# Three low-half subtractions and their sources moved from VectorE and PSUM to GpSimd and SBUF in a recurrence followed by two gated MLPs

## The chip, the cores and the metric

The kernel runs on one core of a Trainium2 chip. The metric is device microseconds of one execution, and a kernel's time is the median of its runs. The engines go by the profile's names: PE is TensorE, DVE is VectorE, ACT is ScalarE, POOL is GpSimd, SP issues most of the DMAs. A name ending in q (SPq, ACTq) is an engine's own instruction queue.

## The reference

```python
state = zeros(B, H, D, D)                       # B, H, S, D = 4, 8, 768, 40
for t in range(S):
    y[t] = einsum('bhd,bhde->bhe', r[t], state)
    Sa = einsum('bhde,bhe->bhd', state, a[t])
    state = state * w[t][:, :, None, :] - outer(Sa, b[t]) + outer(v[t], k[t])
x = y as (3072, 320)
h = x @ w_in                                    # 320 -> 2048
g = where(h >= 1, h, where(h <= -1, 0, (h + 1)**2 / 4))
x = g @ w_out                                   # 2048 -> 320
out = (silu(x @ w_gate) * (x @ w_val)) @ w_out2 # 320 -> 1536 -> 320
```

All inputs and the output are f32.

## The kernel before

**Halves.** TensorE is fed f16. Each f32 operand is cut in a high part (a cast, made by ScalarE) and a low part (the f32 value less the high part, rounded to f16), and three of the four products of halves are summed in f32. So nearly every value that goes into a product costs one copy on ScalarE and, after it, one subtraction on VectorE or GpSimd. GpSimd does it only where the f32 value is in SBUF; where it is in PSUM, VectorE does.

**Chunks.** The 768 time steps are cut into 12 chunks (c = 0 to 11) of 64, and the recurrence of a chunk is turned into matrix products. A unit n = 4c + j is one chunk of one batch element j, with its 8 heads side by side, so there are 48 units. A unit has two parts:
- `p_tasks` (line 821) prepares: loads a, r, k, b and the running products of the decay w, multiplies, splits, transposes, and multiplies keys with a and b (`mm`, line 883) into a PSUM tile pg of 128 x 512 f32. Rows 0 to 63 are masked in place to the strictly triangular part (line 889, VectorE), cast to the f16 high part in lkt (line 904, ScalarE) and subtracted to its low part (line 910, VectorE). Rows 64 to 127 are copied to the SBUF tile gf (line 893) and go through DRAM to the inversion.
- `m_tasks` (line 1011) runs the recurrence: scales v by 256 into its f16 high part vh (line 1053) and makes its low part into vss (line 1057, VectorE by the helper `split`, line 569, 128 x 320); then alternates products and splits (`mm_x`, `mm_sa`, `mm_c`) through a PSUM tile px; transposes vss; multiplies with r (`mm_q`, line 1149) into pg; masks that in place (line 1155, VectorE), casts its high part into wt (line 1159, ScalarE), subtracts its low part into wt (line 1161, VectorE by line 567, 128 x 512); `mm_y` (line 1165) then gives the output y and the next state, which the same unit of the next chunk needs (tiles s0t, s0s). The output is transposed into mx (`turn_x`, line 1006).

`inv_tasks` (line 919) inverts all small triangular blocks of a chunk on VectorE in 62 dependent pairs of steps (lines 949 and 954), in a pg tile that it holds all that while. `decay_tasks` makes the running products of w, for four chunks at a time.

**The MLPs.** Four units of a chunk make 256 tokens. `in1` (8 pieces a chunk) and `in2` (6 pieces) multiply with the input weights (line 1218, PSUM tile ph), apply the activation on ScalarE and VectorE, split the result (line 1238 on ScalarE, then line 1240 on GpSimd by `split`, line 567), and `outp` multiplies with the output weights (line 1285, PSUM tile po). The weights come in as f32 pieces while the kernel runs; `wpiece` (line 612) turns each with three bit operations on VectorE (lines 641, 645, 651), a scaling and a cast on ScalarE (lines 671, 663) and a low-part subtraction on GpSimd or, for the narrow pieces, VectorE. They share buffers (wr, wu) in SBUF.

**What sets the order.** Nothing is written in final order. Every step is handed to `Plan.task` (line 45) with an engine, a cost, what it reads and writes, the buffers that it uses and a priority. `Plan.forward` (line 69) plays the program through with these costs, each engine taking the ready task of best priority, a buffer going to the next user when its last one is done; `Plan.backward` (line 220) does so from the end to get priorities; `Plan.run` (line 320) goes between them `rounds` times and then emits each engine's instructions in the order of the last pass. So every engine's queue has a fixed order made at build time, in which an instruction waits for its inputs and all behind it wait too. Tables of offsets to the priorities by chunk, unit and step (`K.nudge`, `K.last`, lines 1328 to 1430) shape that order. `lk=True` marks VectorE tasks that the planner doesn't play beside a GpSimd task. The numbers of buffers matter here: pg has two PSUM tiles, gf, wt, ldv, ss one each, vh two, vss three; sr, a staging tile for the next state, lies in rows 0 to 39 of gf.

The sets KLP, VLP, L2P, ARP, XSP (lines 382 to 386) name the chunks in which a low part is made by GpSimd (`side`, line 575, picks engine and cost); VLP is empty.

Of the kernel before, what the change touches and what calls it, by code (L numbers as in the profile page):

```python
# [15 lines left out]
class Plan:  # L16
# [10 lines left out]
    def __init__(self):  # L27
        self.tasks, self.made, self.pools, self.slots = [], {}, {}, {}
        self.bias, self.unit, self.nudge, self.last = 0.0, ["z", 0, 0], ({}, {}), ({}, {})
        self.lim, self.rounds, self.loose = 0.73, 2, ()  # L30
# [38 lines left out]
    def forward(self, prio):  # L69
# [59 lines left out]
        while done < len(ts):  # L129
            started = True  # L130
            while started:
                started = False
                for eng in self.ENGINES[:5]:
# [7 lines left out]
                    while any(heaps):  # L141
# [42 lines left out]
                        if t["dma"]:  # L184
                            heapq.heappush(events, (end, -1))
                            dma = max(dma, begin) + t["dma"]
                            end = dma + 1.79
# [32 lines left out]
    def backward(self, prio):  # L220
# [16 lines left out]
        def lat(t):  # L237
            return 1.16 + t["dma"] if t["dma"] else t["lat"]
# [107 lines left out]
def tile_recurrence__then__gated_mlps(  # L346
# [36 lines left out]
    VLP = ()  # L383
    L2P = range(12)
    ARP = range(1, 12)
    XSP = range(12)
    VO = 1
# [58 lines left out]
    K.pool("sr", [gfs[0][0:D].bitcast(F16).rearrange("p h t -> p (h t)")[:, 0:3 * HD].rearrange(  # L446
        "p (l h d) -> p l h d", l=3, h=H)])
    sbt("pf", [128, H, C], F32, 1)
    mx = sbt("mx", [128, 36 * NT], F16)
# [82 lines left out]
    def c_v(n, ps=False):  # L532
        return 0.15 + n * 1.04e-3
# [19 lines left out]
    def hc(ap):  # L553
        return ap.rearrange("p (h t) -> p h t", h=H)
# [266 lines left out]
    def p_tasks(n, p):  # L821
# [61 lines left out]
        def mm():  # L883
# [4 lines left out]
        T("PE", 0.3, mm, r=[(key, "kbT"), ("art", n)], w=[(key, "g")], use=PG + KT + A_ + GF + LK + L2, p=p)  # L888
        T("DVE", c_v(512, True), lambda: v_.tensor_tensor(
            out=hc(G("pg", key))[0:C], in0=hc(G("pg", key))[0:C],  # L890
            in1=mask[0:C].unsqueeze(1).to_broadcast([C, H, C]), op=ALU.mult),
          r=[(key, "g")], w=[(key, "gm")], use=PG, p=p)
# [9 lines left out]
        for hf in range(2):  # L902
            DMA(lambda e, hf=hf: st(e, hf), r=[(key, "gf")], w=[("lsd", c)], use=GF, p=p - 20, dma=0.24, cost=0.68)
        T("ACT", c_s(512), lambda: s_.copy(
            out=G("lkt", key)[0:C, 0:H], in_=hc(G("pg", key))[0:C]),
          r=[(key, "gm")], w=[(key, "lkh")], use=PG + LK, p=p)
# [3 lines left out]
        T("DVE", c_v(512), lambda: v_.tensor_tensor(  # L910
            out=G("lkt", key)[C:128, 0:H], in0=hc(G("pg", key))[0:C],
            in1=G("lkt", key)[0:C, 0:H], op=ALU.subtract), r=[(key, "lkh")], w=[("lk", n)], use=PG + LK, p=p)
# [98 lines left out]
    def m_tasks(n, p):  # L1011
# [15 lines left out]
        if j % 2 == 0:  # L1027
# [24 lines left out]

        T("ACT", c_s(HD), lambda: s_.activation(
            out=G("vh", key), in_=G("ldv", mp)[:, j % 2], func=AF.Copy, scale=2.0**8),
          r=[(mp, "v")], w=[(key, "vh")], use=V + VH, p=p - 1)
        e0, eng, cost = side(c in VLP, HD)
        T(eng, cost, lk=True, emit=lambda: split(
            G("vss", key)[:, :, D:2 * D], G("ldv", mp)[:, j % 2], 2.0**8, G("vh", key), e0),
# [90 lines left out]
        def mm_q():  # L1149
# [4 lines left out]
        T("PE", 0.28, mm_q, r=[(key, "vsT"), ("art", n)], w=[(key, "q")], use=PQ + VT + AT, p=p)  # L1154
        T("DVE", c_v(512, True), lambda: v_.tensor_tensor(
            out=hc(G(pg, (key, "q"))), in0=hc(G(pg, (key, "q"))),
            in1=mask.unsqueeze(1).to_broadcast([128, H, C]), op=ALU.mult),
          r=[(key, "q")], w=[(key, "pf")], use=PQ, p=p)
        T("ACT", c_s(512), lambda: s_.copy(out=G("wt", key)[:, 0, :, 0:C], in_=hc(G(pg, (key, "q")))),
          r=[(key, "pf")], w=[(key, "ph")], use=PQ + WT, p=p)  # L1160
        T("DVE", c_v(512), lambda: split(
            G("wt", key)[:, 1, :, 0:C], hc(G(pg, (key, "q"))), 1.0, G("wt", key)[:, 0, :, 0:C]),
          r=[(key, "ph")], w=[(key, "wt")], use=PQ + WT, p=p)
# [161 lines left out]
    def by(tables):  # L1325
# [248 lines left out]
```

## Time and profile before

| | us |
|---|---|
| median of 3 runs | 1077.28 |
| lowest, highest run | 1075.42, 1082.75 |
| the profiled execution | 1082.65 |
| its span, first to last instruction | 1080.6 |

| engine | busy us | share of the span | instructions |
|---|---|---|---|
| PE | 886.9 | 82% | 10944 |
| DVE | 760.4 | 70% | 1901 |
| ACT | 715.4 | 66% | 1336 |
| POOL | 691.1 | 64% | 912 |

The profiled execution is one run with the hardware profiler on; its span is what the trace shows, and about 2 us lie around it. A busy share is a mean over stretches with different limits, so the rows below go by stretches. PEclk is the clock that TensorE was granted, as a share of full speed. A wait is the idle time of an engine just before an instruction, put down to what came last.

### The profile page before, as it was taken

The numbers are of one execution on the slowest core, as the hardware profiler recorded it, in microseconds if no ns is written. First come the engines' busy times: TensorE is split into PE (matmuls) and PEld (weight loads), VectorE is DVE, ScalarE is ACT, GpSimd is POOL, SyncE is SP. The second block draws the span as 40 slices with busy tenths as digits, with TensorE's granted clock in tenths as the row PEclk, the third lists the DMA queues.
The fourth block names the chain that finished last, engine by engine and source line by source line (L and its number), as shares of the span: only waits on it lengthen the run. The fifth ranks groups of instructions, "written<-read, shape, count | busy, mean of one in ns | idle before, by whom it ended". The sixth has DMA issues, their size and how long they took to land.

```text
span 1080.6 us, 28683 instructions
## 1 busy us (share of the span) xinstructions
PE 886.9 (82%) x10944; PEld 732.9 (68%) x10944; DVE 760.4 (70%) x1901; ACT 715.4 (66%) x1336; POOL 691.1 (64%) x912
## 2 busy tenths in 40 slices
PE   0421326648886999999999999999999999999998
PEld 0311325436764787887878878888888888888887
DVE  8688897999998586884965967848769478441211
ACT  1785676668875967777758768677687674643422
POOL 4588885666887767776766667767668564432222
PEclk9999967769997999999999999999999999999999
DMA  7976798679897897498795875978959462230000
GB/s 224 198 196 158 208 193 178 170 176 230 206 203 143 167 166 136 101 161 151 151 123 119 147 150 115 148 134 161 140 122 162 97 121 58 58 43 20 14 3 25
DMA packets 386193, 147.93 MB, mean 137 GB/s; under 512 B 344536, under 2 KB 362776, under 8 KB 386056
## 3 DMA queue, kind: packets, MB, share of 16 engines
q1 hardware_dynamic: 360118, 133.63, 59.8%
q10 hardware_dynamic: 25938, 12.47, 6.0%
q8 instruction: 86, 1.41, 0.6%
q14 instruction: 51, 0.42, 0.1%
HBM read 78.25 MB, written 21.52 MB: 92 GB/s over the span
## 4 chain that ended last, share of the span: by engine, by line
PE 47%; DVE 26%; DMA 9%; ACT 6%; issue 5%; POOL 3%; SPq 2%; ACTq 0%; DVEq 0%; POOLq 0%
PE ph L1218 25%; PE po L1285 15%; DVE ub L949 3%; DVE pg L954 3%; DVE vss L569 3%; PE pg L1173 2%; DMA tt<-tsd 2%; DVE px L641 1%; DMA mx<-x 1%; DVE mx L1254 1%; PE px L1084 1%; DVE px L645 1%; PE px L1073 1%; PE px L1091 1%; DVE xs L569 1%
## 5 line engine op out<-in xcount | busy, mean ns | idle before, releaser
L1285 PE MATMUL po<-wo,mx 128*128 128x320 f16 x2016 | 314.5, 304 | 11.1 <-ACT wo L663 5.8
L567 POOL TENSOR_TENSOR mx<-mx 128x512 f16<-128x512 f32 x168 | 195.6, 1167 | 175.0 <-ACT mx L1238 168.3
L1285 PEld LDWEIGHTS <-mx 128*128 128x128 f16 x2016 | 191.6, 99 | 80.9 <-issue 7.1
L1218 PE MATMUL ph<-mx,w 128*128 128x256 f16 x1536 | 190.7, 277 | 20.0 <-DMA mx<-x 10.0
L1218 PEld LDWEIGHTS <-w 128*128 128x128 f16 x1536 | 150.0, 99 | 44.7 <-issue 19.5
L1254 DVE SCALAR_TENSOR_TENSOR mx<-ph,mx 128x512 f32<-128x512 f32 x96 | 66.2, 689 | 109.1 <-ACT mx L1251 105.3
L1218 PE MATMUL ph<-x2t,wv 128*128 128x256 f16 x1152 | 141.3, 272 | 1.4 <-DVE mx L1268 1.4
L1218 PE MATMUL ph<-x2t,wg 128*128 128x256 f16 x1152 | 140.3, 272 | 2.2 <-ACT mx L1265 2.2
L1238 ACT CAST mx<-mx 128x512 f16<-128x512 f32 x168 | 102.5, 613 | 54.7 <-DVE mx L1268 29.9
L1218 PEld LDWEIGHTS <-wg 128*128 128x128 f16 x1152 | 110.0, 98 | 17.4 <-issue 2.7
L1218 PEld LDWEIGHTS <-wv 128*128 128x128 f16 x1152 | 109.3, 98 | 14.6 <-issue 1.4
L954 DVE TENSOR_TENSOR pg<-pg,ub 128x126 f32<-128x126 f32 (+22 forms) x372 | 95.7, 257 | 8.2
L949 DVE SCALAR_TENSOR_TENSOR ub<-ub,pg 128x126 f32<-128x126 f32 (+22 forms) x372 | 92.0, 247 | 10.9 <-DMA ub<-lsd 1.1
L1268 DVE SCALAR_TENSOR_TENSOR mx<-ph,mx 128x512 f32<-128x512 f32 x72 | 49.5, 687 | 67.0 <-PE ph L1218 65.5
L1250 ACT ACTIVATE mx<-ph 128x512 f32<-128x512 f32 x96 | 57.1, 595 | 35.4 <-PE ph L1218 32.0
L1116 ACT ACTIVATE vss<-px 32x640 f16<-32x640 f32 x90 | 60.8, 690 | 18.9 <-PE px L1084 14.0
L573 POOL TENSOR_TENSOR ldp<-ldp 128x640 f32<-128x640 f32 (+1 forms) x46 | 70.6, 1545 | 2.6 <-ACT ldp L853 0.6
L1265 ACT ACTIVATE mx<-ph 128x512 f32<-128x512 f32 x72 | 42.7, 594 | 42.8 <-PE ph L1218 38.6
L1107 POOL COPY xs<-xs 32x320 f16<-32x320 f16 x93 | 41.4, 449 | 40.4 <-ACT xs L1102 36.6
L1251 ACT ACTIVATE mx<-mx 128x512 f32<-128x512 f32 x96 | 60.5, 630 | 3.1
L1084 PEld LDWEIGHTS <-tt 96*128 96x128 f16 (+1 forms) x768 | 28.1, 96 | 41.4 <-DMA tt<-tsd 15.0
L569 DVE SCALAR_TENSOR_TENSOR vss<-px,vss 32x320 f16<-32x320 f32 x90 | 43.5, 484 | 16.9 <-ACT vss L1116 13.8
(232 smaller groups left out, 1684.3 us busy)
## 6 DMA issues: line engine op xcount, KB each, us to landing
ub<-lsd SPq DMA_DIRECT2D x24, 256.0 KB
ldp<-in_kb_dram SPq DMA_DIRECT2D x19, 320.0 KB
ldv<-in_v_dram SPq DMA_DIRECT2D x19, 320.0 KB
ldp<-in_ar_dram SPq DMA_DIRECT2D x18, 320.0 KB
wo<-in_wo_dram SPq DMA_DIRECT2D x16, 320.0 KB
waf<-was SPq DMA_DIRECT2D x23, 160.0 KB
out_dram<-mx SPq DMA_DIRECT2D x23, 160.0 KB
ldp<-wks SPq DMA_DIRECT2D x20, 160.0 KB
```

Of the source, the lines that this page charges most:

```text
L567: e.tensor_tensor(out=out, in0=x, in1=hi, op=ALU.subtract)
L569: e.scalar_tensor_tensor(out=out, in0=x, scalar=scale, in1=hi, op0=ALU.mult, op1=ALU.subtract)
L573: e.tensor_tensor(out=out, in0=x, in1=y, op=ALU.mult)
L949: v_.scalar_tensor_tensor(out=t, in0=L()[:, j, j + 1:].unsqueeze(1).to_broadcast([128, nm, ni]), scalar=-(2.0**-10), in1=m[:, 0:nm, j:j + ...
L954: v_.tensor_tensor(out=m[:, 0:nm, j + 1:], in0=m[:, 0:nm, j + 1:], in1=t, op=ALU.add)
L1116: s_.activation(out=hi2(G("vss", key)[z]), in_=two(hd(G("px", key))[32 * hf:32 * hf + 32]), func=AF.Copy, scale=-(2.0**-10))
L1218: t_.matmul(out=ps, lhsT=wts[:, wi, fs], rhs=xT[:, xi, :], start=(i == 0), stop=(i == len(plan) - 1))
L1238: T("ACT", c_s(512) - 0.04, lambda: s_.copy(out=G("g", key)[:, 0], in_=u2(key)), r=[(key, "u")], w=[(key, "gh")], use=U + GG, p=p)
L1250: s_.activation(out=u2(key), in_=ps2(key), func=AF.Relu, scale=2.0**-8, bias=1.0)
L1251: s_.activation(out=u2(key), in_=u2(key), func=AF.Square, scale=2.0**3)
L1254: T("DVE", c_v(512, True), lambda: v_.scalar_tensor_tensor(out=u2(key), in0=ps2(key), scalar=2.0**8, in1=u2(key), op0=ALU.max, op1=ALU.min ...
L1285: t_.matmul(out=ps, lhsT=g[:, x, f, 128 * tt:128 * tt + 128], rhs=wo[:, 2 * i + f, y, :], start=(n == 1 and f == 0 and m == 0), stop=(n == ...
```

## The change

The low part of v (chunks 1 to 11), of the masked key product (chunks 2 to 11) and of the masked r product (chunks 1 to 11) is made by GpSimd in place of VectorE. GpSimd can't take the masked products from PSUM, so VectorE's mask multiplication writes them to SBUF (rows 0 to 63 of gf; a new tile qf of 128 x 512 f32), and ScalarE's cast reads them there. For v, ScalarE multiplies the loaded pair of units by 256 in place, once for two units, so that the low part is a plain subtraction. The staging tile sr moves from gf to unused rows of ss. Beside that, the planner's numbers change: `lim` 0.73 to 1.13, `rounds` 2 to 4, two DMA latencies, and all four tables of offsets are replaced.

```diff
--- before.py
+++ after.py
@@ -27,7 +27,7 @@
     def __init__(self):
         self.tasks, self.made, self.pools, self.slots = [], {}, {}, {}
         self.bias, self.unit, self.nudge, self.last = 0.0, ["z", 0, 0], ({}, {}), ({}, {})
-        self.lim, self.rounds, self.loose = 0.73, 2, ()
+        self.lim, self.rounds, self.loose = 1.13, 4, ()
 
     def pool(self, name, tiles):
         self.pools[name] = dict(free=list(tiles), users={}, spares=[], grow=[])
@@ -184,7 +184,7 @@
                         if t["dma"]:
                             heapq.heappush(events, (end, -1))
                             dma = max(dma, begin) + t["dma"]
-                            end = dma + 1.79
+                            end = dma + 1.94
                         else:
                             end += t["lat"]
                         heapq.heappush(events, (end, i))
@@ -235,7 +235,7 @@
         now, done, starts, held, events, size = 0.0, 0, [0.0] * len(ts), set(), [], len(ts)
 
         def lat(t):
-            return 1.16 + t["dma"] if t["dma"] else t["lat"]
+            return 1.44 + t["dma"] if t["dma"] else t["lat"]
 
         seen = set()
 
@@ -380,10 +380,12 @@
     NDC = 2
     NPM = 1
     KLP = range(1, 12)
-    VLP = ()
+    VLP = range(1, 12)
     L2P = range(12)
     ARP = range(1, 12)
     XSP = range(12)
+    WTP = range(1, 12)
+    LKP = range(2, 12)
     VO = 1
     WSP = True
     NW1 = 14
@@ -443,9 +445,10 @@
     sbt("xs", [128, H, D], F16, 2)
     tts = sbt("tt", [128, 4 * H * HC + C], F16, 1)
     gfs = sbt("gf", [128, H, C], F32, 1)
-    K.pool("sr", [gfs[0][0:D].bitcast(F16).rearrange("p h t -> p (h t)")[:, 0:3 * HD].rearrange(
+    K.pool("sr", [ss[0][0:D].rearrange("p h t -> p (h t)")[:, 0:3 * HD].rearrange(
         "p (l h d) -> p l h d", l=3, h=H)])
     sbt("pf", [128, H, C], F32, 1)
+    sbt("qf", [128, H, C], F32, 1)
     mx = sbt("mx", [128, 36 * NT], F16)
     K.pool("xt", [mx[:, 6 * NT * i:6 * NT * (i + 1)].rearrange("p (a t) -> p a t", a=6)
                   for i in range(2)])
@@ -886,10 +889,13 @@
                 t_.matmul(out=ps[:, h], lhsT=kT[0:120, h, :], rhs=at[0:120, h, 0:C])
 
         T("PE", 0.3, mm, r=[(key, "kbT"), ("art", n)], w=[(key, "g")], use=PG + KT + A_ + GF + LK + L2, p=p)
+        lkp = c in LKP
+        gm = lambda: G("gf", key)[0:C] if lkp else hc(G("pg", key))[0:C]
+        GM = GF if lkp else PG
         T("DVE", c_v(512, True), lambda: v_.tensor_tensor(
-            out=hc(G("pg", key))[0:C], in0=hc(G("pg", key))[0:C],
+            out=gm(), in0=hc(G("pg", key))[0:C],
             in1=mask[0:C].unsqueeze(1).to_broadcast([C, H, C]), op=ALU.mult),
-          r=[(key, "g")], w=[(key, "gm")], use=PG, p=p)
+          r=[(key, "g")], w=[(key, "gm")], use=PG + GM, p=p)
         T("ACT", c_s(512), lambda: s_.activation(
             out=G("gf", key)[C:128], in_=hc(G("pg", key))[C:128], func=AF.Copy, scale=2.0**-6),
           r=[(key, "g")], w=[(key, "gf")], use=PG + GF, p=p)
@@ -901,15 +907,15 @@
 
         for hf in range(2):
             DMA(lambda e, hf=hf: st(e, hf), r=[(key, "gf")], w=[("lsd", c)], use=GF, p=p - 20, dma=0.24, cost=0.68)
-        T("ACT", c_s(512), lambda: s_.copy(
-            out=G("lkt", key)[0:C, 0:H], in_=hc(G("pg", key))[0:C]),
-          r=[(key, "gm")], w=[(key, "lkh")], use=PG + LK, p=p)
+        T("ACT", c_s(512), lambda: s_.copy(out=G("lkt", key)[0:C, 0:H], in_=gm()),
+          r=[(key, "gm")], w=[(key, "lkh")], use=GM + LK, p=p)
         T("ACT", c_s(256), lambda: s_.copy(
             out=G("l21", key)[64:96, 1:1 + H], in_=G("gf", key)[64:96, :, HC:C]),
           r=[(key, "gf")], w=[(key, "l2h")], use=GF + L2, p=p)
-        T("DVE", c_v(512), lambda: v_.tensor_tensor(
-            out=G("lkt", key)[C:128, 0:H], in0=hc(G("pg", key))[0:C],
-            in1=G("lkt", key)[0:C, 0:H], op=ALU.subtract), r=[(key, "lkh")], w=[("lk", n)], use=PG + LK, p=p)
+        e3, eng, cost = side(lkp, 512)
+        T(eng, cost, lambda: e3.tensor_tensor(
+            out=G("lkt", key)[C:128, 0:H], in0=gm(),
+            in1=G("lkt", key)[0:C, 0:H], op=ALU.subtract), r=[(key, "lkh")], w=[("lk", n)], use=GM + LK, p=p)
         e2, eng, cost = side(c in L2P, 256)
         T(eng, cost, lk=True, emit=lambda: split(
             G("l21", key)[96:128, 1:1 + H], G("gf", key)[64:96, :, HC:C], 1.0,
@@ -1050,12 +1056,19 @@
                 out=tiles(64, 96), in_=td[0].rearrange("s f b t -> s f (b t)")),
                 r=[("tsd", c)], w=[(mp, "tt")], use=TT, p=p - 3, dma=0.25, cost=0.68)
 
+        vscale = 2.0**8
+        if c in VLP:
+            vscale = 1.0
+            if j % 2 == 0:
+                T("ACT", c_s(2 * HD), lambda: s_.activation(
+                    out=G("ldv", mp), in_=G("ldv", mp), func=AF.Copy, scale=2.0**8),
+                  r=[(mp, "v")], w=[(mp, "v8")], use=V, p=p - 2)
         T("ACT", c_s(HD), lambda: s_.activation(
-            out=G("vh", key), in_=G("ldv", mp)[:, j % 2], func=AF.Copy, scale=2.0**8),
-          r=[(mp, "v")], w=[(key, "vh")], use=V + VH, p=p - 1)
+            out=G("vh", key), in_=G("ldv", mp)[:, j % 2], func=AF.Copy, scale=vscale),
+          r=[(mp, "v8" if c in VLP else "v")], w=[(key, "vh")], use=V + VH, p=p - 1)
         e0, eng, cost = side(c in VLP, HD)
         T(eng, cost, lk=True, emit=lambda: split(
-            G("vss", key)[:, :, D:2 * D], G("ldv", mp)[:, j % 2], 2.0**8, G("vh", key), e0),
+            G("vss", key)[:, :, D:2 * D], G("ldv", mp)[:, j % 2], vscale, G("vh", key), e0),
           r=[(key, "vh")], w=[(key, "vl")], use=V + VH + VS, p=p - 1)
         copy, eng, cost = (p_.tensor_copy, "Pool", c_ps(2 * HD)) if c >= VO else (s_.copy, "ACT", c_s(2 * HD))
         T(eng, cost, emit=lambda: copy(
@@ -1152,15 +1165,18 @@
                 t_.matmul(out=ps[:, h], lhsT=vT[0:120, h, :], rhs=at[0:120, h, C:128])
 
         T("PE", 0.28, mm_q, r=[(key, "vsT"), ("art", n)], w=[(key, "q")], use=PQ + VT + AT, p=p)
+        wtp = c in WTP
+        qm = lambda: G("qf", key) if wtp else hc(G(pg, (key, "q")))
+        QM = [("qf", key)] if wtp else PQ
         T("DVE", c_v(512, True), lambda: v_.tensor_tensor(
-            out=hc(G(pg, (key, "q"))), in0=hc(G(pg, (key, "q"))),
+            out=qm(), in0=hc(G(pg, (key, "q"))),
             in1=mask.unsqueeze(1).to_broadcast([128, H, C]), op=ALU.mult),
-          r=[(key, "q")], w=[(key, "pf")], use=PQ, p=p)
-        T("ACT", c_s(512), lambda: s_.copy(out=G("wt", key)[:, 0, :, 0:C], in_=hc(G(pg, (key, "q")))),
-          r=[(key, "pf")], w=[(key, "ph")], use=PQ + WT, p=p)
-        T("DVE", c_v(512), lambda: split(
-            G("wt", key)[:, 1, :, 0:C], hc(G(pg, (key, "q"))), 1.0, G("wt", key)[:, 0, :, 0:C]),
-          r=[(key, "ph")], w=[(key, "wt")], use=PQ + WT, p=p)
+          r=[(key, "q")], w=[(key, "pf")], use=PQ + QM, p=p)
+        T("ACT", c_s(512), lambda: s_.copy(out=G("wt", key)[:, 0, :, 0:C], in_=qm()),
+          r=[(key, "pf")], w=[(key, "ph")], use=QM + WT, p=p)
+        e4, eng, cost = side(wtp, 512)
+        T(eng, cost, lambda: split(G("wt", key)[:, 1, :, 0:C], qm(), 1.0, G("wt", key)[:, 0, :, 0:C], e4),
+          r=[(key, "ph")], w=[(key, "wt")], use=QM + WT, p=p)
 
         def mm_y():
             ps, wq, kb, at = hd(G(pg, (key, "y"))), G("wt", key), G("kbs", pk), G("art", pk)
@@ -1326,106 +1342,91 @@
         return {(u, i): x for u, table in tables.items() for i, x in table.items()}
 
     by_chunk = by({
-        "a": {9: -0.16, 10: 2.53, 11: -1.57},
...
+        "z": {0: 16.32},
...
```


## Rows read from the trace of the kernel before

**Rows 1.** Busy time of the engines in five stretches of the span, us.

```profile
core 0: us, PE busy (x) PEld busy (x) DVE busy (x) ACT busy (x) POOL busy (x), PEclk, DMA share, GB/s
0.00:160.00 160.00, 41.21 (x592) 34.60 (x593) 134.90 (x387) 99.02 (x167) 115.57 (x228) 0.94 0.80 196
160.00:340.00 180.00, 124.61 (x1524) 97.88 (x1524) 162.81 (x384) 129.37 (x248) 124.83 (x154) 0.82 0.82 191
340.00:372.00 32.00, 28.88 (x337) 23.06 (x336) 17.35 (x39) 26.08 (x48) 26.41 (x36) 0.96 0.76 144
372.00:840.00 468.00, 454.94 (x5926) 380.39 (x5924) 349.62 (x879) 344.09 (x656) 334.70 (x397) 1.00 0.77 141
840.00:1080.00 240.00, 237.24 (x2572) 197.00 (x2569) 95.74 (x216) 116.81 (x221) 89.61 (x100) 1.00 0.24 48
```

**Rows 2.** The same columns, the second stretch cut in two.

```profile
160.00:196.00 36.00, 20.09 (x216) 16.03 (x216) 27.83 (x70) 20.89 (x40) 21.81 (x36) 0.74 0.91 194
196.00:340.00 144.00, 104.52 (x1309) 81.85 (x1308) 134.99 (x315) 108.48 (x209) 103.03 (x118) 0.84 0.80 191
```

**Rows 3.** VectorE's groups by shape, 160 to 340 us: operation, count, busy us, mean ns.

```profile
L569 DVE SCALAR_TENSOR_TENSOR vss<-ldv,vh 128x320 f16<-128x320 f32 x8 | 6.2, 779 | 0.4 <-DMA vsT<-vss 0.3
...
L567 DVE TENSOR_TENSOR wt<-pg,wt 128x512 f16<-128x512 f32 x8 | 5.5, 685 | 0.1
...
L910 DVE TENSOR_TENSOR lkt<-pg,lkt 64x512 f16<-64x512 f32 x7 | 4.8, 684 | 0.9 <-ACT lkt L904 0.7
```

**Rows 4.** VectorE's groups by shape, 0 to 160 us.

```profile
L910 DVE TENSOR_TENSOR lkt<-pg,lkt 64x512 f16<-64x512 f32 x8 | 5.4, 683 | 1.3 <-ACT lkt L904 1.1
...
L910 DVE TENSOR_TENSOR lsp<-pg,lsp 64x512 f16<-64x512 f32 x2 | 1.4, 684 | 1.1 <-ACT lsp L904 1.0
```

**Rows 5.** The tile ldv: one operation's shortest, median and longest ns.

```profile
L569 DVE SCALAR_TENSOR_TENSOR vss<-ldv,vh x48: 473/675/2681, 21.8 to 939.8; 128x320 f16<-128x320 f32 x48
```

**Rows 6.** Groups of the whole span: operation, count, busy us, mean ns, idle before.

```profile
L567 POOL TENSOR_TENSOR mx<-mx 128x512 f16<-128x512 f32 x168 | 195.6, 1167 | 175.0 <-ACT mx L1238 168.3 <-POOL vss L1098 2.5 <-issue 1.2
...
L567 POOL TENSOR_TENSOR ars<-ldp,ars 128x320 f16<-128x320 f32 x44 | 35.5, 807 | 8.7 <-ACT ars L865 4.5 <-issue 1.8 <-POOL vss L1098 0.5
...
L1238 ACT CAST mx<-mx 128x512 f16<-128x512 f32 x168 | 102.5, 613 | 54.7 <-DVE mx L1268 29.9 <-DVE mx L1254 14.6 <-DMA x2t<-mx 4.9
...
L865 ACT ACTIVATE ars<-ldp 128x640 f16<-128x640 f32 x45 | 33.0, 733 | 5.7 <-POOL ldp L573 4.5 <-DMA art<-ars 0.6
...
L569 DVE SCALAR_TENSOR_TENSOR xs<-px,xs 32x320 f16<-32x320 f32 x89 | 42.5, 482 | 13.4 <-ACT xs L1102 11.1
...
L1254 DVE SCALAR_TENSOR_TENSOR mx<-ph,mx 128x512 f32<-128x512 f32 x96 | 66.2, 689 | 109.1 <-ACT mx L1251 105.3 <-PE px L1084 1.8 <-PE pg L1173 1.5
...
L1155 DVE TENSOR_TENSOR pg<-pg,mask 128x512 f32<-128x512 f32 x44 | 30.5, 693 | 2.3 <-PE pg L1152 1.9
...
L1159 ACT CAST wt<-pg 128x512 f16<-128x512 f32 x44 | 25.7, 584 | 15.9 <-DVE pg L1155 15.2
```

**Rows 7.** What TensorE waited for, 160 to 340 us: total us, times, longest.

```profile
PE po L1285 <- ACT wo L663: 5.8, 1, 5.8
...
PE pg L1173 <- DVE wt L567: 3.7, 2, 3.1
...
PE pg L886 <- DVE wt L567: 2.7, 1, 2.7
```

**Rows 8.** Line 1007's transposes into mx: first and last start, us.

```profile
L1007 SPq DMA_TRANSPOSE mx<-x x24: 1211/1244/2527, 144.3 to 971.3; - x24
```

**Rows 9.** The chain of waits: start us, us, what.

```profile
168.00 3.58 PE ph L1218 x16
...
1063.73 3.49 PE ph L1218 x32
...
1067.23 1.63 PE po L1285 x12
```

**Rows 10.** What GpSimd waited for, 372 to 840 us.

```profile
POOL mx L567 <- ACT mx L1238: 45.5, 29, 7.5
```

More of the change, by code (lines that the diff above doesn't have):

```diff
@@ L1328, in tile_recurrence__then__gated_mlps @@
     by_chunk = by({
[22 rows of a table removed]
+        "a": {0: 0.7, 11: -0.75},
+        "b": {3: 0.07, 5: -0.15, 7: 1.48, 8: -0.07, 10: 2.42, 11: 7.11},
+        "d": {0: 5.17, 1: 4.15, 2: 3.13},
+        "i": {0: -2.35, 1: -1.77, 2: -1.74, 3: -0.61, 4: 2.98, 6: 1.13, 7: 3.24, 8: 2.28, 9: 3.28, 10:
+            7.81, 11: 4.67},
+        "o": {0: 49.18},
+        "p": {15: 0.02, 16: 0.55, 17: 0.02, 18: 0.02, 19: 0.02, 20: 0.02},
+        "v": {3: 0.77, 16: 0.81, 17: 0.81},
+        "w": {0: 0.8, 1: 0.03, 2: -0.74, 3: -1.52, 4: -2.29, 5: -3.06, 6: -3.84, 7: -4.61},
+        "z": {0: 16.32},
     })
     by_step = by({
[14 rows of a table removed]
[12 rows of a table added]
     })
```

160 rows, old and new, of tables (by_chunk, by_step) are left out of this document.

## The prediction

> **What bounds the kernel now.** I read the busy times by stretch first, because the page's shares (PE 82%, DVE 70%) are means over stages with different limits. From 372 us to the end TensorE is the bound: it is busy 454.9 of 468 us and then 237.2 of 240 [rows 1], and the chain of waits there is its own matmuls [rows 9]. All that any other engine can still give back there is 468 - 454.9 = 13.1 us, and 2.8 after it. From 160 to 340 us TensorE is busy only 124.6 of 180 us, at a granted clock of 0.82; the time lost is 55 us. There VectorE is the fullest engine, 162.8 of 180, and cut in two it has 27.8 of 36 and then 135.0 of 144, 94% [rows 1, 2]. ACT has 72%, GpSimd 69%, the DMA engines 82%. So in that stretch the work that feeds TensorE (the recurrence of chunks 1 and 2, the weights of the second MLP, the inversions) goes at VectorE's pace. TensorE's longest wait there, 5.8 us for a weight cast in wo [rows 7], is of this kind: ACT had that cast to make late, because VectorE's bit operations on the piece came late in a full queue. From 0 to 160 us VectorE is busy 134.9, but the change moves almost nothing there, as chunk 0 keeps its form.
>
> The end of the kernel is therefore the point at which TensorE becomes full, plus matmul work that the change leaves alone. What is won ahead of 340 us is won at the end, and what is won on VectorE after 372 us is worth next to nothing.
>
> **The change, part by part.** The sum goes against the profiled execution, 1082.65 us (span 1080.6 and 2.05 around it). It lies 5.4 above the median of the runs, at their upper end, so I take the difference from the median, 1077.28.
>
> *VectorE loses, ahead of 340 us.* The low part of v: 8 instructions, 6.2 us. The low part of the masked r product: 8, 5.5 us. The low part of the masked key product: 7, 4.8 us [rows 3]. Before 160 us there are 10 of the last kind [rows 4], of which 8 belong to chunks 0 and 1 and stay; 2 x 0.684 = 1.4 us. Together 17.9 us. In the fullest part VectorE has only 6% of idle time to swallow this, so I count 17 us of it as time.
>
> The low part of v takes 0.779 us each there, from 0.473 to 2.681 over the kernel [rows 5], where a subtraction as wide with one operand in PSUM takes 0.482 [rows 6]. I count the 0.779 as freed, since the queue behind it stood still for that long. The Trainium skill (SBUF — State Buffer, "Who interferes with whom") says that a VectorE instruction with two SBUF inputs and a GpSimd instruction that reads SBUF lock each other out, the later one waiting for the whole of the other; the trace agrees with it in the 2.681 us. By that rule the surplus is real queue time; at the unblocked 0.482 the 17.9 would be 15.5.
>
> *GpSimd gains.* A two-input subtraction of 512 takes it 1.167 us, of 320 it takes 0.807 [rows 6]. Ahead of 340 us that is 8 x 0.807 + 17 x 1.167 = 26.3 us, nearly all after 160: its share goes from 69% to some 83%. It has the room. But two of the three are on chains: wt is what `mm_y` waits for, and each is 1.167 - 0.685 = 0.48 us longer, plus a wait in a fuller queue, for which I take half an instruction, 0.6 us. Eight units make 8.6 us if every one is on the path. TensorE had idle time before the r product's consumer put down to the wt low part for 3.7 us in 2 waits, and for the pg tile that it frees in one of 2.7 [rows 7], so about 3 of 8 units count: 3.2 us. Bounds: 0 and 8.6.
>
> *VectorE's masks* now write to SBUF in place of PSUM. A 128 x 512 instruction from PSUM to SBUF takes 0.689 and one from PSUM to PSUM 0.693 [rows 6]: nothing.
>
> *ScalarE.* Its casts read SBUF: 0.613 against 0.584 [rows 6], 15 x 0.03 = 0.4 us. The scaling of v in place is a new 128 x 640 instruction; the nearest row is 0.733 [rows 6]; 4 pairs ahead of 340 us make 2.9 us. ScalarE has 50 us idle in the stretch and v is loaded well ahead, so both cost nothing; if that cover went, 3.3 us.
>
> *Buffers.* A pg tile is free after its mask and one copy, no longer after a cast and a subtraction: earlier by 0.58 + 0.68 us. That is worth from nothing to the 2.7 us of the wait named above; I take half, 1.3. Against it, gf (one tile) is held until GpSimd has made the key's low part, where it was held until its two DMAs to DRAM had read it; the next unit's key product waits for gf. Mask, cast and subtraction make 0.69 + 0.58 + 1.17 = 2.4 us after the product, and the same time runs for the copy and the DMAs, so I take nothing; at worst it is 7 x 0.6 = 4 us. The staging tile sr leaves gf, which takes a user off it. ldv (one pair) and vh wait for GpSimd where they waited for VectorE: 0.03 us more per instruction, plus its queue.
>
> *DMAs* stay the same in number and size; SP issues the same.
>
> *The new order.* All tables and two constants of the planner change, so every queue is ordered anew. No row shows a price. Its upper end is what a better order could find: 160 - 134.9 = 25.1 us of VectorE idle time before 160 us, of which half, 12.5, might be had, and some of the 13.1 after 372. Its lower end I take at the same 13.1 us lost. I put it at nothing and keep both ends for the range.
>
> Sum: -17 + 3.2 - 1.3 = -15. The profiled execution would become 1068 and the median **1062**.
>
> **The rivals.**
>
> *GpSimd becomes the pace (slower).* From 372 to 840 us it is busy 334.7 of 468 [rows 1]. Of the 44, 44 and 40 units of the three kinds, 36, 36 and 31 are left after 340 us; they take 36 x 0.807 + 67 x 1.167 = 107 us and lie between 340 and 971, where the recurrence ends [rows 8], so 468/631 of them, 80 us, fall in that stretch: 414 of 468, 89%. The 133 us that it idles now are not all free: 45.5 of them it waits for the f16 cast that its own MLP subtraction needs [rows 10]. If it can use only a third of them, 44, it falls 36 us behind, and the outcome is -15 + 36: 1098. The point of decision is a share of 85%, (334.7 + 80 - 15) / 468: if its queue can't get beyond that, the loss eats the whole gain. For it: every one of TensorE's output products waits for a GpSimd subtraction. Against it: the last transpose of the recurrence starts 109 us before the end, while chunk 11's own MLPs take 8 x (1.75 + 1.63) + 6 x (3.49 + 1.63) = 58 us by the durations of [rows 9]. TensorE has 51 us of other work in hand by then, so a recurrence that falls back by less than that leaves it full; and after 840 us GpSimd has only 89.6 of 240 to do. VectorE ran at 94% in order, so 89% can be had. The Trainium skill (GPSIMD Engine Reference, "Engine selection") advises against just this move: elementwise work belongs on VectorE, as GpSimd is about 2 times slower with two inputs. The rows have 1.167 against 0.685, 1.7 times. By the rule the move is a loss of engine time, and it is one of time here only if this rival holds. Chance 0.13.
>
> *VectorE is not what paces the stretch (no change).* The loads of the weights and the decays, 82% of the DMA engines [rows 1], or the recurrence's own latency would then set the time, and VectorE would only idle more. The chain loses 3.2 us more, the order gives or takes a few: 1071 to 1083, centre 1078. For it: the first 36 us of the stretch have the DMA engines at 0.91 and VectorE at 77% [rows 2]. Against it: the 94% of the 144 us after. Chance 0.27.
>
> *The new order pays by itself (faster still).* With half of the 25.1 us before 160: 1062 - 12.5 = 1050. Chance 0.10.
>
> **How the numbers follow.** My forecast has 0.50, with a range of its own of 1056 to 1071: 17.9 with no loss on the chains against 17.9 x 0.9 with 8.6 lost. The likeliest time is 1062. The 8 in 10 range is 1047 to 1082: it leaves out the slower case (0.13) and the low half of the last one (0.05). A measurement of this kernel tells about 1% from no change, so the borders are 1066.5 and 1088. Faster: 0.42 of the forecast's 0.50, the 0.10, and 0.01 of the flat case, 0.53. Same: 0.08, 0.26 and 0.01 of the slow case, 0.35. Slower: 0.12.
>
> **What would show it.** VectorE's busy time should fall by 34 + 30 + 27 us (44 units at 0.779, 44 at 0.685, 40 at 0.684), about 92, and GpSimd's rise by some 134 (44 x 0.807 + 84 x 1.167); ScalarE's by 16. The windows from 196 to 340 us should show VectorE still the fullest but with more TensorE time inside, a higher granted clock there, and TensorE full from about 357 in place of 372. GpSimd's share from 372 to 840 should stand near 89% with TensorE still at 97%. I am wrong if the first MLP matmul of the new kernel (now at 168 [rows 9]) has moved by more than 5 us, as then the order and not the load made the difference; if VectorE's share before 340 falls and TensorE's point of fullness stays; or if TensorE shows waits for GpSimd's subtractions after 372 us that add up to more than 10 us.

## The result and the profile after

The changed kernel takes **1068.4 us** (median of 4 runs, 1067.38 to 1069.65) against 1076.69 us for the kernel before in runs beside it: a ratio of 0.9906, 95% interval 0.9881 to 0.993. That is 8.3 us less, where 15 were forecast; the time lies in the forecast range, 6.4 us above its centre, and on the "within 1%" side of the border, though the interval reaches across it.

The profiled execution of the changed kernel took 1068.32 us (span 1066.6), close to its median. The one of before lies 5.4 us above its median, so the two traces differ by 14.0 us of span, and some 5 to 6 of these are not the change. The trace can't say in which stretch those lie.

Busy time of the whole span, from the page of the changed kernel:

```profile
PE 881.3 (83%) x10944; PEld 730.6 (68%) x10944; DVE 683.1 (64%) x1773; ACT 734.7 (69%) x1358; POOL 812.0 (76%) x1040
```

Its busy times by stretch, in the columns of [rows 1] and [rows 2] (the last stretch ends with the span):

```profile
0.00:160.00 160.00, 39.53 (x560) 33.36 (x560) 139.93 (x389) 99.42 (x169) 115.66 (x224) 1.00 0.79 205
160.00:340.00 180.00, 124.52 (x1551) 97.00 (x1552) 145.15 (x356) 132.03 (x249) 150.86 (x185) 0.87 0.83 185
340.00:372.00 32.00, 29.83 (x347) 23.53 (x345) 15.54 (x33) 26.08 (x48) 25.72 (x36) 0.98 0.59 126
372.00:840.00 468.00, 464.69 (x6061) 391.49 (x6059) 302.87 (x819) 365.71 (x685) 422.98 (x490) 1.00 0.77 145
840.00:1066.00 226.00, 222.69 (x2432) 185.24 (x2430) 79.58 (x180) 111.49 (x209) 96.78 (x107) 1.00 0.20 44
...
160.00:196.00 36.00, 18.36 (x231) 14.88 (x232) 24.16 (x68) 23.76 (x46) 31.64 (x48) 1.00 0.73 164
196.00:340.00 144.00, 106.16 (x1326) 82.11 (x1323) 121.00 (x289) 108.27 (x204) 119.22 (x138) 0.84 0.85 190
```

Two things stand against each other here. From 160 to 340 us VectorE has 17.7 us less to do, where the forecast took 16.5 off this stretch, and falls from 94% to 84% of the last 144 us. As it does 5.0 more ahead of 160 us, it has 12.6 less up to 340, where 17.9 were forecast. But TensorE does no more in that stretch: 124.5 us where [rows 1] has 124.6, and 2111 matmuls by 340 us where it had 2116. The gain is elsewhere: from 372 to 840 us TensorE idles 3.3 us instead of 13.1.

The stores of the output say the same chunk by chunk (start, us; the MLP planes of one chunk end with them). SyncE's timeline of the kernel before, chunks 0, 1, 3, 6 and 10:

```profile
351.16 0.54 SPq L1310 DMA_DIRECT2D out_dram<-mx  x1
354.47 0.53 SPq L1310 DMA_DIRECT2D out_dram<-mx  x1
...
424.48 0.74 SPq L1310 DMA_DIRECT2D out_dram<-mx  x1
...
572.51 0.38 SPq L1310 DMA_DIRECT2D out_dram<-mx  x1
...
787.43 1.26 SPq L1310 DMA_DIRECT2D out_dram<-mx  x2
...
1054.05 0.81 SPq L1310 DMA_DIRECT2D out_dram<-mx  x2
```

The same of the changed kernel:

```profile
353.54 0.85 SPq L1326 DMA_DIRECT2D out_dram<-mx  x2
...
423.70 0.53 SPq L1326 DMA_DIRECT2D out_dram<-mx  x1
...
563.59 2.33 SPq L1326 DMA_DIRECT2D out_dram<-mx  x1
...
772.08 0.35 SPq L1326 DMA_DIRECT2D out_dram<-mx  x1
...
1039.53 24.46 SPq L1326 DMA_DIRECT2D out_dram<-mx  x4
```

Chunk 0 leaves at about the same time in both; then the gap grows to 15 us by chunk 6 (787.43 against 772.08) and stays. Some 6 us of it can be that the profiled execution of before lies above its median. So the forecast named a gain ahead of 340 us and next to nothing behind it, and the trace shows the reverse.

Why does a lighter VectorE not bring chunk 0 out earlier? One difference stands ahead of it: the first MLP matmul, at 168.00 in [rows 9], starts 12 us later. The changed kernel's timeline of TensorE:

```profile
180.19 1.86 PE L1234 MATMUL ph<-mx,w 128*128 128x256 f16 x8 [3.45 <-DMA mx<-x]
```

and what TensorE waited for up to 182 us (total us, times, longest), first:

```profile
PE ph L1097 <- DMA tt<-tsd: 22.2, 1, 22.2
PE pg L889 <- DVE wg L757: 9.8, 1, 9.8
```

then from 160 to 340 us, in the columns of [rows 7]:

```profile
PE px L1104 <- POOL vss L1111: 6.0, 1, 6.0
...
PE px L1097 <- DVE xs L572: 4.5, 4, 2.2
PE po L1189 <- ACT wt L1175: 4.1, 1, 4.1
PE pg L1189 <- ACT wt L1175: 4.1, 1, 4.1
PE ph L1234 <- DVE wv L572: 3.9, 1, 3.9
```

The 22.2 us for chunk 0's own inverted matrix were 11.0 before, and the matrix comes at 118.6 us in place of 111.1. The 9.8 us are put down to a copy for the decays; a_no_low below, which has the same order, has 8.5 us at that place and puts them down to the transposed keys (`kbT<-kbs`), so that name isn't sure. From the first MLP matmul to the last store of chunk 0 it is now 353.5 - 180.2 = 173.3 us, where it was 354.5 - 168.0 = 186.5: 13 us won in between, and 12 lost ahead of it. That one ate the other isn't shown: in the orders tried below the first store doesn't follow this start. That VectorE does 139.9 us ahead of 160, 5.0 more than before, is the order too, as the change moves almost nothing there. The waits for VectorE's wt [rows 7] are gone. The longest of them ended at 231.6 us; at 231.8 us there is now a wait of 4.1 us for the ScalarE cast one step ahead (the other 4.1 us, in po, are chunk 0's, which the change leaves alone).

The rows for the moved subtractions, GpSimd's groups by shape from 160 to 340 us, against VectorE's in [rows 3]:

```profile
L916 POOL TENSOR_TENSOR lkt<-gf,lkt 64x512 f16<-64x512 f32 x9 | 10.4, 1151 | 2.5 <-ACT lkt L910 1.9
L570 POOL TENSOR_TENSOR wt<-qf,wt 128x512 f16<-128x512 f32 x8 | 9.3, 1156 | 0.6 <-ACT wt L1175 0.6
...
L570 POOL TENSOR_TENSOR vss<-ldv,vh 128x320 f16<-128x320 f32 x9 | 7.1, 790 | 1.5 <-ACT vh L1066 0.8 <-DMA vsT<-vss 0.7
```

The tile ldv in the changed kernel, where [rows 5] has 473/675/2681:

```profile
L570 POOL TENSOR_TENSOR vss<-ldv,vh x44: 784/792/799, 142.2 to 925.4; 128x320 f16<-128x320 f32 x44
L1063 ACT ACTIVATE ldv<-ldv x22: 719/732/738, 138.4 to 883.7; 128x640 f32<-128x640 f32 x22
```

And what GpSimd waits for from 372 to 840 us, where [rows 10] has 45.5:

```profile
POOL mx L570 <- ACT mx L1254: 7.4, 12, 1.3
```

### The profile page after: what moved, and what is told of

It is laid out like the page before. It is cut to its first block, busy times and chain, and to the rows that moved or that the text cites. A ratio compares the mean times of both kernels' runs of the same rounds, so it can differ in the third digit from the quotient of the medians.

```text
span 1066.6 us, 28811 instructions
## 1 busy us (share of the span) xinstructions
PE 881.3 (83%) x10944; PEld 730.6 (68%) x10944; DVE 683.1 (64%) x1773; ACT 734.7 (69%) x1358; POOL 812.0 (76%) x1040
## 5 line engine op out<-in xcount | busy, mean ns | idle before, releaser
L1301 PE MATMUL po<-wo,mx 128*128 128x320 f16 x2016 | 310.8, 300 | 4.2 <-POOL wo L570 2.2
L1234 PE MATMUL ph<-mx,w 128*128 128x256 f16 x1536 | 194.1, 277 | 6.3 <-DMA mx<-x 3.5
L1234 PE MATMUL ph<-x2t,wg 128*128 128x256 f16 x1152 | 142.8, 275 | 2.8 <-POOL wg L570 1.4
L572 DVE SCALAR_TENSOR_TENSOR xs<-px,xs 32x320 f16<-32x320 f32 x88 | 42.3, 483 | 34.4 <-ACT xs L1115 32.4
```

The costliest lines, as they stand in the source:

```text
L572: e.scalar_tensor_tensor(out=out, in0=x, scalar=scale, in1=hi, op0=ALU.mult, op1=ALU.subtract)
L1234: t_.matmul(out=ps, lhsT=wts[:, wi, fs], rhs=xT[:, xi, :], start=(i == 0), stop=(i == len(plan) - 1))
L1301: t_.matmul(out=ps, lhsT=g[:, x, f, 128 * tt:128 * tt + 128], rhs=wo[:, 2 * i + f, y, :], start=(n == 1 and f == 0 and m == 0), stop=(n == ...
```

## The experiments

Every kernel was timed in turns with the kernel before on the same chip; the ratio is to that, and times of rows with different values for the kernel before compare by their ratios. "Placement" means which engine makes the three low parts, "tables" the planner's offsets (by chunk and by step), "constants" its two latencies of a transfer (1.79 and 1.16 us, now 1.94 and 1.44) and its limits. "Store" is the start of the first store of chunk 0, us (351.2 in the kernel before, 353.5 in the changed kernel).

| kernel | us (before beside it) | ratio, 95% | store |
|---|---|---|---|
| a_all_dve | 1114.24 (1078.43) | 1.0333, 1.0294 to 1.0372 | 370.3 |
| b_all_pool | 1111.79 (1078.43) | 1.0307, 1.026 to 1.0353 | 354.3 |
| a_oldtab | 1086.76 (1078.43) | 1.0067, 1.0043 to 1.0091 | 349.8 |
| a_plan_dve | 1125.9 (1078.43) | 1.0432, 1.039 to 1.0474 | 368.7 |
| z_pool_new | 1088.79 (1078.19) | 1.0098, 1.0063 to 1.0132 | 357.2 |
| z_dve_new | 1101.44 (1078.19) | 1.0212, 1.0185 to 1.0239 | 367.6 |
| z_pool_old | 1082.3 (1078.19) | 1.0031, 1.0014 to 1.0047 | 357.2 |
| z_dve_old | 1089.91 (1078.19) | 1.0108, 1.0083 to 1.0133 | 362.0 |
| b_no_low | 1070.26 (1080.88) | 0.9898, 0.9865 to 0.9931 | 346.7 |
| b_twice | 1148.94 (1080.88) | 1.0616, 1.0581 to 1.065 | 371.6 |
| a_wt_dve | 1085.36 (1080.88) | 1.0035, 1.0017 to 1.0052 | 357.4 |
| a_no_low | 1065.65 (1080.88) | 0.9853, 0.9823 to 0.9882 | 351.0 |

**The work alone, in an order that isn't its own.** Theory "load": the relief of VectorE makes the gain, whatever the order. Rival "order": the new order makes it.

a_all_dve keeps the order of the changed kernel and issues its three low parts to VectorE:

```
+        e3 = v_
...
+        e0 = v_
...
+        e4 = v_
```

> The changed kernel with every queue in its own order, but the three low parts issued to VectorE in place of GpSimd (92 us back on VectorE, 134 off GpSimd; the sources stay in SBUF). Theory 'load' (the gain is VectorE's relief): the gain is gone, 1076 us or more, up to 1090 as the order was made for a lighter VectorE. Theory 'order' (the gain is the new order of the queues): within 4 us of the changed kernel, 1064 to 1072.

b_all_pool keeps the order of the kernel before and makes the three low parts on GpSimd, from SBUF copies:

```
-            G("wt", key)[:, 1, :, 0:C], hc(G(pg, (key, "q"))), 1.0, G("wt", key)[:, 0, :, 0:C]),
+            G("wt", key)[:, 1, :, 0:C], qm(), 1.0, G("wt", key)[:, 0, :, 0:C],
+            p_ if c else v_),
...
```

> The kernel before with every queue in its own order, but the same three low parts issued to GpSimd from SBUF copies (and v scaled once per pair). Theory 'load': faster than before by most of the predicted 15 us, 1060 to 1070, and chunk 0's output store, at 354 us in both kernels, comes 10 us earlier. Theory 'order': no gain, 1074 to 1085, since GpSimd's queue was not ordered for the added work.

Both missed. The new order with VectorE's placement is 4.3% slower than the changed kernel (1.0333 against 0.9906); the old order with GpSimd's placement loses 33.4 us against the kernel before. In b_all_pool VectorE is relieved as forecast, and TensorE waits for GpSimd instead. Its busy times from 160 to 340 and from 372 to 840 us (columns of [rows 1]):

```profile
160.00:340.00 180.00, 122.16 (x1508) 95.95 (x1508) 148.54 (x350) 131.60 (x251) 148.53 (x179) 0.84 0.80 189
372.00:840.00 468.00, 440.20 (x5617) 364.79 (x5616) 279.60 (x748) 340.03 (x636) 386.18 (x449) 0.99 0.70 132
```

and its longest sum of waits of TensorE from 372 to 840 us, a row that isn't in the changed kernel, where no wait of TensorE in that stretch is over 1.0 us:

```profile
PE pg L1191 <- POOL wt L574: 15.4, 14, 2.4
```

So GpSimd's wt does stand on the path, where nothing in the order makes room for it. In a_all_dve wt also costs VectorE 810 ns for 684, now that it is subtracted from SBUF, but the three together cost it only 3 us more than before. Neither theory alone holds. The third one, "fit", is that an order is only good for the placement that it was made for.

**The tables and constants alone.** a_oldtab plans the new placement with the tables and constants of before; a_plan_dve plans the old placement with the new ones:

```
-    VLP = range(1, 12)
+    VLP = ()
...
-    WTP = range(1, 12)
-    LKP = range(2, 12)
+    WTP = ()
+    LKP = ()
...
```

> The changed kernel planned with the offsets, rounds, window and DMA latencies of the kernel before: new placement, old tables. Theory 'load': 1066 to 1074. Theory 'order': 1076 or more.

> The changed kernel with its own tables and constants, planned anew with the three sets of chunks empty, so that the low parts are VectorE's and the planner knows it: old placement, new tables. Theory 'load': 1076 to 1090. Theory 'order': 1066 to 1072.

a_oldtab is 8 us slower than before, where "order" had it; a_plan_dve is 47 slower, beyond what either had. The tables are offsets fitted to one placement, and the new ones do nothing good for the old placement: "the new order pays by itself" falls.

**No tables at all.** To see the placement without a fit, every offset table is emptied and four kernels cross placement (pool: new, dve: old) with constants (new, old). The two of a pair differ in placement alone, and neither order was fitted to either.

```
-    by_chunk = by({
-        "a": {0: 0.7, 11: -0.75},
...
```

> The changed kernel planned with all tables of offsets empty and its own constants: the new placement in an order that no table was made for. Its partner is the old placement planned the same way. Theory 'relief' (VectorE's 92 us less are worth time in any order that knows of them): 10 to 20 us faster than the partner. Theory 'fit' (the gain is in tables that fit a placement): within 8 us of the partner, and both 20 us or more slower than the kernel before.

> The old placement (three sets empty) planned with empty tables and the changed kernel's constants; partner of the one before. Theory 'relief': 10 to 20 us slower than the partner. Theory 'fit': within 8 us.

> The new placement planned with empty tables and the constants of the kernel before (rounds 2, window 0.73, latencies 1.79 and 1.16). Theory 'relief': 10 to 20 us faster than its partner. Theory 'fit': within 8 us of it.

> The old placement planned with empty tables and the constants of the kernel before; partner of the one before. Theory 'relief': 10 to 20 us slower than the partner; theory 'fit': within 8 us.

The placement is worth 1101.44 - 1088.79 = 12.7 us with the new constants, as "relief" had it, and 1089.91 - 1082.3 = 7.6 with the old, just inside the 8 of "fit". The 20 us behind the kernel before, which "fit" also wanted, only z_dve_new has. Here the forecast mechanism is to be seen. From 160 to 340 us with the new constants, VectorE's placement and then GpSimd's:

```profile
160.00:340.00 180.00, 115.42 (x1452) 90.70 (x1453) 151.63 (x349) 123.35 (x234) 118.79 (x148) 0.81 0.79 179
```

```profile
160.00:340.00 180.00, 126.22 (x1527) 97.81 (x1528) 145.54 (x354) 126.70 (x238) 145.86 (x183) 0.88 0.80 177
```

TensorE is busy 10.8 us more, with 75 matmuls more (8.3 us and 40 with the old constants), and chunk 0's first store comes 10.4 us earlier (4.8 with the old). The tables then bring the old placement from 1089.9 to 1078.2 and the new one from 1088.8 (new constants) to 1068.4: 12 and 20 us. But without tables the new constants are themselves slower, by 6.5 us for the new placement and 11.5 for the old. From z_dve_old the steps to the changed kernel are -7.6 for the placement, +6.5 for the constants and -20 for the tables, and by another path they would be others: the gain can't be shared out between the parts.

**How much the relief is worth in before's own order.** b_no_low leaves the three low parts out of the kernel before once their buffers are filled; b_twice makes each of them twice. The order of all else is before's. Both touch the 128 subtractions that the change moves, and both go through one helper; where b_no_low has `0 == 2`, b_twice has `2 == 2`.

```
+    def lowdo(on, name, key, do):
+        x = (name, id(G(name, key)))
+        if 0 == 2 and on:
+            do()
+        if 0 == 2 or not on or x not in seen:
+            do()
+        seen.add(x)
...
-        T("DVE", c_v(512), lambda: split(
+        T("DVE", c_v(512), lambda: lowdo(c, "wt", key, lambda: split(
...
```

> The kernel before in its own order, the three low parts left out from the point where their buffers have once been filled (so the output lacks them): VectorE does some 88 us less and GpSimd nothing more. Theory 'relief' (VectorE paces the front in the order of before): chunk 0's output store comes 12 to 17 us before 354 us and the time is 1055 to 1064. Theory 'fit' (that order has the front's waits elsewhere): the store stays within 4 us of 354, the time above 1066.

> The kernel before in its own order, each of the three low parts made twice by VectorE (92 us more on it). Theory 'relief': chunk 0's output store 15 us later than 354 us, the time 1094 to 1110. Theory 'fit': the store within 4 us, the time below 1090.

Taking the work away, at no cost on any other engine, brings 10.6 us, and 4.5 of them ahead of chunk 0's store. Doubling it costs 68 us, 20 of them there. So the three subtractions on VectorE are felt steeply upward and weakly downward. As each of them is also a link in a chain (`mm_y` waits for wt), both runs change the length of that chain with the load, and nothing here parts the two. b_no_low's time is longer than "relief" wanted and its store moved by less; "fit" has its time, and misses its store by half a microsecond. b_twice fits neither, being slower than both had it. What is late next shows in b_no_low's waits of TensorE from 160 to 340 us, beside those of [rows 7]:

```profile
PE ph L1228 <- DMA mx<-x: 8.0, 2, 7.0
PE px L1094 <- DVE xs L579: 5.7, 3, 2.6
PE po L1295 <- ACT wo L673: 4.8, 1, 4.8
...
PE pg L1183 <- ACT wt L1169: 3.1, 1, 3.1
PE pg L896 <- ACT wt L1169: 1.9, 1, 1.9
```

The waits for the wt low part, 3.7 + 2.7 us, are gone, and 3.1 + 1.9 us for the cast ahead of it have come, ahead of the same matmuls. The wait for the weight cast in wo went only from 5.8 to 4.8, and the one for VectorE's xs stays (5.8 before). VectorE is now busy 123.9 of the 144 us from 196 to 340:

```profile
196.00:340.00 144.00, 105.30 (x1267) 81.78 (x1268) 123.93 (x303) 108.14 (x211) 104.00 (x127) 0.86 0.84 190
```

It has 11.1 us less to do there than in [rows 2], and TensorE is busy 0.8 more. More of the gain lies behind: the lead on the kernel before grows from 4.5 us at chunk 0's store to 11.6 at chunk 6's (775.8 against 787.4), and TensorE idles 9.3 us from 372 to 840, where it idled 13.1:

```profile
372.00:840.00 468.00, 458.66 (x5954) 384.67 (x5952) 301.44 (x812) 345.71 (x657) 329.75 (x396) 1.00 0.77 142
```

In b_twice the first row of TensorE's waits from 372 to 840 us is the low part itself:

```profile
PE pg L1183 <- DVE wt L577: 19.0, 15, 2.7
```

**One part back, and GpSimd relieved.** a_wt_dve returns the low part of wt alone to VectorE, in the changed kernel's order:

```
         e4, eng, cost = side(wtp, 512)
+        e4 = v_
```

> The changed kernel in its own order, only the low part of the masked r product issued to VectorE again (from SBUF). If the longer chain through GpSimd costs time, it is up to 5 us faster than the changed kernel; if the order wants its own placement, a third of what all three cost, 10 to 18 us slower (1078 to 1086).

a_no_low leaves the three low parts out of the changed kernel, nearly all of what the change gave to GpSimd:

```
-        T(eng, cost, lambda: split(G("wt", key)[:, 1, :, 0:C], qm(), 1.0, G("wt", key)[:, 0, :, 0:C], e4),
+        T(eng, cost, lambda: lowdo(wtp, "wt", key, lambda: split(
...
```

> The changed kernel in its own order, the three low parts left out once their buffers have been filled (the output lacks them): GpSimd does some 125 us less. If GpSimd paces the changed kernel from 372 us on, 10 us faster or more (below 1058). If TensorE is the bound there, the gain is at most the idle time that is left ahead of 372 us and on the chains: 1060 to 1068.

One part of three in the wrong place costs about 14 us by the ratios, 1.0035 against 0.9906, as was said for an order that wants its own placement. It isn't the order alone, though. From SBUF, beside GpSimd, VectorE takes 0.921 us for a subtraction that took 0.684 from PSUM, 10 us in all:

```profile
L570 DVE TENSOR_TENSOR wt<-qf,wt 128x512 f16<-128x512 f32 x44 | 40.5, 921 | 3.7 <-ACT wt L1175 3.2
```

No such cost stands in a_plan_dve, which subtracts from PSUM in a new order and is the slowest of the crossed kernels. In a_no_low GpSimd falls to 340.4 us from 372 to 840, and TensorE stays where it was, at 464.4 against 464.7:

```profile
372.00:840.00 468.00, 464.43 (x6027) 391.01 (x6026) 301.49 (x815) 364.44 (x684) 340.40 (x406) 1.00 0.77 145
```

Its ratio of 0.9853 against 0.9906 has intervals that just touch (0.9882 and 0.9881). At most half a per cent is GpSimd's, and the trace puts it ahead of chunk 0's store (351.0 against 353.5).

## Why the prediction was right, and where it was not

**VectorE's work: right.** The three groups should lose about 92 us. They lost 35.8 + 30.1 + 27.3 = 93.2. The page has 77.3 less: the records of its instructions sum to 808.4 us before and 721.9 after, so they overlapped by 9.2 us more before, and some subtractions of weights take longer now (last section). GpSimd's rise was 120.9 for 134 forecast, ScalarE's 19.3 for 16.

**"I count 17 us of it as time": this step failed in size.** The argument was that an engine at 94% has only 6% of idle time to swallow a relief. b_no_low gives that relief for nothing, and shortens the chain to `mm_y` besides: 4.5 us at the first store and 10.6 at the end. The orders without tables give 4.8 and 10.4 us at that store and 7.6 and 12.7 at the end. The gain is real and goes with the work taken off VectorE, though load and chain aren't parted, and it passes at a quarter to about 60% ahead of the store, not at 95%. 94% busy wasn't the same as pacing: in a fixed order the same stretch holds waits on ScalarE's casts and on the transfers of chunk 0, and these stayed or moved up when VectorE's went.

**"Worth next to nothing" on VectorE after 372 us: this step failed.** The same relief in before's own order, b_no_low, takes TensorE's idle time there from 13.1 to 9.3 us, by one trace of each, and more of its gain lies behind chunk 0's store than ahead of it.

**"The new order at nothing": this step failed, in both directions.** In the changed kernel the front shows no gain at all. Its order starts the first MLP matmul 12 us later. The changed order with GpSimd relieved, a_no_low, starts it at 179.6 us, and the order of before with VectorE relieved, b_no_low, at 165.0: that start goes with the order and not with the load. The prediction had set that as a sign that it would be wrong (moved by more than 5 us), and it came. Behind 372 us the changed kernel takes away 9.8 of TensorE's 13.1 idle microseconds, which the text put at nothing; the stores show the gap open between chunks 1 and 6. Of these the relief alone has 3.8 (b_no_low), and the new placement with the old tables, a_oldtab, has none: it idles 13.8. TensorE's busy time after 372 us is also 4.8 us less, for as many matmuls (8498 and 8493). Idle and busy make up the 14 us between the traces; how much of each is the profiled execution of before lying 5.4 above its median can't be told. So the sum came out near the measured time partly by two errors of opposite sign.

**The wt chain through GpSimd, +3.2: smaller.** In the changed kernel TensorE waits 1.7 us in all for wt's subtraction, in 2 waits, none of them after 372 us. In b_all_pool it waits 15.4 us from 372 to 840 us alone. The price depends on the order, and only the order made for it hides it.

**Masks and ScalarE: as said; buffers open.** The masks take 0.68 to 0.69 us and the scaling 0.732, for 0.733 taken; TensorE's waits from 372 to 840 us hold 0.6 us for gf and 0.2 for the low part of v. The 1.3 us taken for pg tiles that come free sooner weren't measured by themselves.

**The rivals.** "GpSimd becomes the pace" is false: its share from 372 to 840 us is 90%, where 89% was worked out, past the 85% named as the point of decision, and TensorE idles less than before. Its 45.5 us of waits for the cast shrank to 7.4: the idle time could be used almost whole. a_no_low shows that freeing it changes nothing there. "VectorE doesn't pace the stretch" is half true: 0.25 to 0.6 of its load comes through. "The new order pays by itself" is false, by a_oldtab and a_plan_dve; what does pay is an order fitted to its placement, 12 us for the old one and 20 for the new, each with its own constants.

**Open:** why the fitted order leaves TensorE so little idle time behind 372 us, why it starts the first MLP later, and whether an order that doesn't could have both gains. Across these kernels that start lies anywhere from 163 to 189 us, and the first store doesn't follow it (168.1 and 357.2 in z_pool_new, 163.3 and 362.0 in z_dve_old). What holds chunk 0 back in before's order once VectorE is relieved wasn't separated further.

## What to carry to other kernels

Moving work off the fullest engine is worth what the next wait in each queue leaves of it: look up, for each wait that goes, the step just ahead of it, and price the relief by the gap between the two, not by the engine's busy share. In a kernel whose queues are planned ahead, a placement and its order are one change: measured apart, each half here was slower than both the kernel before and the kernel after. Idle time of a few per cent on the bound engine, spread over many chunks, can be as large as the whole gain (9.8 us here), so it belongs in the forecast as a term. And an instruction moved back to its old engine isn't the old instruction if its operands lie elsewhere: here it took 0.921 us for 0.684.

## What the runs showed of the hardware

GpSimd ran at 90% for 468 us, and TensorE waited 0.2 us for it there, with two-input subtractions that take 1.156 us for VectorE's 0.685. The Trainium skill (GPSIMD Engine Reference, "Engine selection") advises against it for such work; the trace agrees with its price, 1.7 times here for about 2. The advice isn't borne out for an engine that had 133 of 468 us idle: without tables, the placement on GpSimd is faster by 7.6 and by 12.7 us.

VectorE and GpSimd lengthen each other's subtractions where both read SBUF. The v subtraction took VectorE 473 to 2681 ns [rows 5]; on GpSimd all 44 lie between 784 and 799 ns. Other instructions of GpSimd do lengthen. In the kernel before, a subtraction of weights on VectorE, which takes 0.685 us in most of its records, starts just behind one of GpSimd and takes 1.63; GpSimd's next one starts within it and takes 1.60, where the median of these 168 is 1.157:

```profile
303.51 1.16 POOL L567 TENSOR_TENSOR wv<-wo,wv 128x512 f16<-128x512 f32 x1
303.58 1.63 DVE L569 SCALAR_TENSOR_TENSOR wv<-lsp,wv 64x512 f16<-64x512 f32 x1
...
304.63 1.60 POOL L567 TENSOR_TENSOR mx<-mx 128x512 f16<-128x512 f32 x1
```

In the changed kernel this falls on what VectorE still subtracts from SBUF: its ten subtractions of weights took 8.0 us before and take 13.1 now. Two of the three long ones stand beside GpSimd work that both kernels have, so the order has its part in that. The longest has three GpSimd instructions wholly inside it, the moved wt and v subtractions among them:

```profile
232.17 3.33 DVE L572 SCALAR_TENSOR_TENSOR wv<-wo,wv 64x512 f16<-64x512 f32 x1 [1.22 <-ACT wv L666]
```

The Trainium skill (SBUF — State Buffer, "Who interferes with whom") has the later of two such instructions wait for the whole of the other; the records of both engines agree.

A fixed order of instructions answered these subtractions unevenly: 91 us of them taken off VectorE brought 10.6 us, 99 us more cost 68.
